# Counting matmuls that take four token tiles at once, and VectorE work moved into gaps, in an attention-plus-MoE kernel

## The chip, the cores and the metric

The kernel runs on one core of a Trainium2 chip. The metric is the device time of one execution in microseconds (us). Before the change it was run three times: 507.22, 510.45 and 506.15 us, median 507.22 us.

## The reference

The input is q, k and v for 4 batches, 8 heads, 768 positions and 64 dimensions. A token attends to a window of 31 positions around it and to the maxima and means of all 24 blocks of 32 keys and values. The result, 3072 tokens of 512 numbers, goes into a mixture of 8 experts in which every expert takes exactly 384 tokens:

```python
logits = x @ w_gate                        # 3072 x 8
for idx in np.argsort(-logits.flatten()):  # best pair first
    tok, e = idx // E, idx % E
    if assigned[tok] >= 0 or counts[e] >= cap:   # cap = 384
        continue
    assigned[tok] = e; counts[e] += 1
for e in range(E):
    out[assigned == e] = np.maximum(x[assigned == e] @ w1[e], 0.0) @ w2[e]
```

The greedy assignment is what makes the work sequential: which tokens an expert gets depends on which experts filled up before it.

## The kernel before, in words

**Stages.** Attention with its logits runs from the start to about 147 us. Then follow eight experts, one after another, each over the 384 tokens of the expert that fills up in that round. The order of the experts is thus found at run time: round r names the expert that is the next to fill up and the tokens it gets, and `widx` (where its weights lie) and `idx` (its token numbers) steer the loads of its weights and the gather of its tokens.

**A round** (`route`, L468). `aim` (L111) takes each token's best remaining logit (`best`), its expert (`oh`, one-hot) and a sortable integer `key`, all on VectorE, and `compare` (L103) makes the 0/1 table `g` of keys against 32 or 64 pivots. `search` (L444) then finds, digit by digit, the pivot at which the first expert reaches 384 tokens. For one digit it does: 24 counting matmuls on TensorE (L449; for each tile of 128 tokens, a 128-column slice of `g` is the stationary operand and the tile's 8 columns of `oh` move through, all added up in `pc`), a VectorE comparison with 384 (`full`, L451), one matmul with `steps` (L454), new pivots (L458) and the next `compare` (L460). A round has two searches of three digits, six digits in all, two of them of width 64 and four of width 32. Round 7, the last, needs no search. After the search come the running counts (`inc`, L508), a prefix matmul (`px`, L522), `place` (L529), the interval tables `span` (L546), 12 small matmuls (`at`, L554) and `idx` (L559). `spent` takes the tokens that are used up out of `WA`, and `close` (L510) takes the full expert out of the logits `L`.

**An expert** (`expert`, L738). Float32 products are made of three float32r products: each operand is split in a high part (ScalarE, `hi`, `xh`, `hh`) and a low part (VectorE, `lo`, `xl`, `hl`). 96 matmuls of 384 columns (L749) give `h`, 72 of 512 columns (L766) give `y`. The weights of the next expert are split in chunks of 128x1024 (`split_w`, L584; low part L594) and its gathered tokens are turned by TensorE in four `flip_x` (L614; the matmuls show as L135), each of which writes the one PSUM buffer `xt`, which is free again when ScalarE has read `xh` (L625) and VectorE `xl` (L628).

**What sets the order.** TensorE and VectorE each work through their instructions in the order in which the program issues them. That order is written by a small clock in the program: `spend` (L664) adds an estimate for each expert matmul to `now`; `service` issues the low parts that are due and then, if `ready` has come, lets `route` go on by one step (`advance`, L651). Each `yield` of `route` gives an estimate of the step's time on TensorE and of the VectorE work that must be over before the next step. So the matmuls of round r+1 are strewn among the matmuls of expert r and before. Rounds run ahead of the experts as far as these estimates let them. Low parts that are due go on the list `later` and are issued when their time has come, whatever VectorE is to do next. Round 0 (L705) runs by itself, before the first expert; three `advance` steps of round 1 stand between the turns of the first expert's tokens (L719).

```python
pc = R[:, :E]
for t in range(NT):                                       # L448
    nc.tensor.matmul(pc, g[t // HT][:, t % HT * n:t % HT * n + 128], oh[:, t], start=t == 0, stop=t == NT - 1)
full = rt.tile([128, E + 1], BF, name="full", bufs=2)
nc.vector.tensor_scalar(full[:, :E], pc, CAP - 0.5, 0.0, op0=OP.is_ge, op1=OP.max, accum_out=full[:, E:])
```

Of the 128 columns of the slice only the first n belong to tile t; the other rows of `pc` are not used.

Of the kernel before, what the change touches and what calls it, by code (L numbers as in the profile page):

```python
# [35 lines left out]
TUNE = dict(  # L36
    hop=0.22, dv=1.0, e5=2, e50=0, warm2=3.6192, adv=14, y0=2.6, y1=0.3, y2=0.45,
    y2m=0.021, y3=1.7, y4=1.5, y5=1.6, y7=1.1, lo=1.1, sp=1.6, qx=23.421, aw=9.0, as_=2.6,
# [18 lines left out]
def attention_moe(ctx, tc, qT, kT, v65, wg, w1r, w2r, cst, out, dbg=None, dbi=None):  # L57
# [14 lines left out]
    ids_b = cb[:, :2 * NT].rearrange("p (t k) -> p t k", k=2)  # L72
    steps = consts.tile([128, len(STEPS), 128], BF, name="steps")
    wgs = consts.tile([128, 4, E], F32, name="wgs")
    L = consts.tile([128, NT, E], F32, name="L")
# [34 lines left out]

    def aim(T, t0, t1, last=False):  # L111
        n = t1 - t0
        best, cand, tgt = T["best"][:, t0:t1], T["cand"][:, t0:t1], T["tgt"][:, t0:t1]
        nc.vector.tensor_reduce(best, L[:, t0:t1], axis=AX.X, op=OP.max)
        ranks, experts = [], [
            lambda: nc.vector.tensor_tensor(cand, L[:, t0:t1], best[:, :, None].to_broadcast([128, n, E]), op=OP.is_equal),
            lambda: nc.vector.tensor_tensor(cand, cand, WA[:, t0:t1], op=OP.mult),
            lambda: nc.vector.tensor_reduce(tgt, cand, axis=AX.X, op=OP.max),
            lambda: nc.vector.tensor_scalar(tgt, tgt, 0.5, None, op0=OP.max)]
        if not last:  # L120
            m, key = T["m"][:, t0:t1], T["key"][:, t0:t1]
            bits = T["best"].bitcast(I32)[:, t0:t1]
            ranks = [
                lambda: nc.vector.tensor_scalar(m, bits, 31, 0x7FFFFFFF, op0=OP.arith_shift_right, op1=OP.bitwise_and),
                lambda: nc.vector.scalar_tensor_tensor(key, bits, 0x8000, m, op0=OP.bitwise_xor, op1=OP.bitwise_xor),
                lambda: nc.vector.tensor_copy(T["dup"][:, t0:t1], T["halves"][:, t0:t1, 1:2].to_broadcast([128, n, 2])),
                lambda: compare(T["g"], T["dup"], T["piv"], T["digits"][0], t0, t1)]
            experts.append(lambda: nc.vector.tensor_tensor(T["oh"][:, t0:t1], cand, tgt[:, :, None].to_broadcast([128, n, E]), op=OP.is_equal))
        for pair in zip_longest(ranks, experts):
            for op in pair:  # L130
                if op:
                    op()

# [43 lines left out]
    with ExitStack() as att:  # L177
# [13 lines left out]

        nc.vector.memset(steps, 0.0)
        for i, (v, n) in enumerate(STEPS):
            nc.vector.memset(steps[:n, i], v)
# [22 lines left out]
        @task("tables", "pool", 3.5, ["constants2"], 1)  # L217
        def _():
            nc.gpsimd.tensor_copy(cb, XS[0][:, :TB])
            nc.gpsimd.tensor_copy(WA, w8f[:, None].to_broadcast([128, NT, E]))  # L220
            nc.gpsimd.tensor_copy(piv0, offs[:, :32])
            nc.gpsimd.tensor_copy(colsi, XS[0][:, TB:TW])
            nc.gpsimd.tensor_copy(pivw, offs[:, 128:192])

        def halves(t):
# [218 lines left out]
    def search(R, oh, dup, g, digits):  # L444
        below = -32768.0 - 65536.0 / digits[0]
        for i, n in enumerate(digits):
            pc = R[:, :E]
            for t in range(NT):  # L448
                nc.tensor.matmul(pc, g[t // HT][:, t % HT * n:t % HT * n + 128], oh[:, t], start=t == 0, stop=t == NT - 1)  # L449
            full = rt.tile([128, E + 1], BF, name="full", bufs=2)  # L450
            nc.vector.tensor_scalar(full[:, :E], pc, CAP - 0.5, 0.0, op0=OP.is_ge, op1=OP.max, accum_out=full[:, E:])  # L451
            yield 0.027 * NT, TUNE["y1"]
            ps = R[:, 16:17 + E]
            nc.tensor.matmul(ps, steps[:, STEP[digits][i]], full, start=True, stop=True)  # L454
            if i < 2:
                m = digits[i + 1]
                piv = rt.tile([128, 64], I16, name="piv", bufs=2)
                nc.vector.tensor_scalar(piv[:, :m], offs[:, FROM[digits][i]:FROM[digits][i] + m], ps[:, E:], below, op0=OP.add, op1=OP.add)  # L458
# [7 lines left out]
    ROUND = {}  # L466

    def route(r):  # L468
        T = first
        if r:  # L470
            T = targets(r)
            aim(T, 0, NT, r == E - 1)
            yield 0.0, TUNE["y0"]
        R = psum.tile([128, 512], F32, name="r")
# [40 lines left out]

        late = TUNE["e5"] if r else TUNE["e50"]
        if r < E - 1 and not late:
            close()
        ROUND[r] = [widx, None]
        yield 0.03, TUNE["y4"]  # L520
        px = R[:, 32:34]
# [9 lines left out]
        def spent():  # L531
            if r == E - 1:
                return
            if late == 1:
                close()
# [27 lines left out]
        if r < E - 1 and late == 2:  # L563
            close()
# [19 lines left out]
    def split_w(r, nm, j, n=1, wait=TUNE["wlo"]):  # L584
# [4 lines left out]
        for k in range(n):  # L589
            c = slice(k * 1024 // n, (k + 1) * 1024 // n)  # L590
            nc.scalar.activation(hi[:, c], raw[:, c], AF.Copy)  # L591

            def low(c=c):
                nc.vector.tensor_tensor(lo[:, c], raw[:, c], hi[:, c].bitcast(F32), op=OP.subtract)  # L594
# [18 lines left out]

    def flip_x(r, d):  # L614
        pt = psum.tile([128, 3, 128], F32, name="xt")
        for c in range(3):
            flip4(pt[:, c], XG[r, c][:, d * 128:(d + 1) * 128])
        split_x(r, d, pt)

    def split_x(r, d, pt):  # L620
# [6 lines left out]
        def low():  # L627
            nc.vector.tensor_tensor(xl[:, d], p, xh[:, d].bitcast(F32), op=OP.subtract)  # L628
            vector(0.55)
        later.append((state["now"] + TUNE["xlo"], low))  # L630

# [3 lines left out]

    def flush():
        for it in later[:]:
            later.remove(it)
            it[1]()

    def service():
        while True:
            for it in [x for x in later if x[0] <= state["now"]]:
                later.remove(it)
                it[1]()
# [92 lines left out]
    def expert(r):  # L738
# [3 lines left out]
        hl = ff.tile([128, 8, CAP], F32R, name="hl")  # L742
        for f in range(8):
            ph = psum.tile([128, CAP], F32, name="h", bufs=3)
            wh, wl = (w.rearrange("p (j d k) -> p j d k", j=2, d=4)[:, f % 2] for w in WT[r, "a", f // 2])
# [9 lines left out]
            def low(f=f, ph=ph):  # L755
                nc.vector.scalar_tensor_tensor(hl[:, f], ph, 0.0, hh[:, f].bitcast(F32), op0=OP.max, op1=OP.subtract)  # L756
                vector(0.55)
            later.append((state["now"] + TUNE["lo"], low))
            if f % 2 == 0:
                later.append((state["now"] + TUNE["sp"], lambda f=f: split_w(r, "b", f // 2)))  # L760
        py = [psum.tile([128, DM], F32, name="y", bufs=3) for c in range(3)]
# [84 lines left out]
```

## Time and profile before

| | us |
|---|---|
| device time of the profiled execution | 508.25 |
| its span, first to last instruction | 506.5 |
| so outside the span | 1.75 |
| median of the three runs | 507.22 |
| TensorE busy in the span | 463.3 |
| VectorE busy in the span | 330.1 |

The mean granted TensorE clock was 0.95 of full speed. In the views below a row of the timeline gives the start and the length in us, the engine, the line, the operation, what it writes and reads, how many instructions were merged, and in brackets how long the engine was idle before and what released it. A row of the chain gives start, length, engine, what is written, and line. Matmuls overlap: the time that one takes out of the stream is the difference of starts, not the length shown.

### The profile page before, as it was taken

What the parts mean: (1) busy time and instruction counts of PE and PEld (TensorE: products, weight loads), DVE (VectorE), ACT (ScalarE), POOL (GpSimd) and SP (SyncE); (2) the same over time, 40 slices, a digit from 0 to 9 for tenths busy, and PEclk for the clock granted to TensorE, in tenths of its full rate; (3) what the DMA queues carried; (4) which work ended last, traced back from release to release, by engine and by line L of the source; (5) the groups of instructions that cost most, each with busy time, mean ns of one, the idle gap of its engine ahead of it and who ended that gap; (6) DMA issues with size and microseconds to landing.
All of it is one profiled execution on the core that took longest, in us unless ns stands there. A gap on an engine that the chain in (4) does not pass through costs nothing.

```text
span 506.5 us, 13149 instructions
## 1 busy us (share of the span) xinstructions
PE 463.3 (91%) x5160; PEld 388.6 (77%) x5160; DVE 330.1 (65%) x1293; ACT 214.4 (42%) x450; POOL 131.7 (26%) x199
## 2 busy tenths in 40 slices
PE   3799999999973899989989999899999999999993
PEld 2568687877853798779768878877987998988982
DVE  3278789977866786757865966777778462362510
ACT  1277667876810441243323513342351453453410
POOL 9547743614220300220202302300400500402011
PEclk8799999999985699979998999999999999999997
DMA  8999969211110821920641733723535445531001
GB/s 264 315 303 297 320 221 312 91 51 44 65 65 6 295 96 38 323 98 1 231 167 63 249 146 104 272 84 154 180 109 184 127 162 169 180 111 42 22 21 41
DMA packets 24157, 76.28 MB, mean 151 GB/s; under 512 B 3488, under 2 KB 3744, under 8 KB 23712
## 3 DMA queue, kind: packets, MB, share of 16 engines
q1 hardware_dynamic: 18336, 56.58, 33.9%
q0 software_dynamic: 5760, 18.88, 10.7%
q8 instruction: 40, 0.66, 0.6%
q14 instruction: 21, 0.17, 0.1%
HBM read 62.86 MB, written 12.58 MB: 149 GB/s over the span
## 4 chain that ended last, share of the span: by engine, by line
PE 73%; DVE 13%; issue 7%; POOL 4%; DMA 1%; ACT 0%; POOLq 0%; SPq 0%; ACTq 0%; DVEq 0%
PE h L749 21%; PE y L766 19%; PE o L348 5%; PE t L135 5%; PE s L312 5%; PE r L449 5%; PE x L135 2%; PE x L269 2%; PE l L354 2%; PE xt L135 2%; POOL vw L204 2%; DVE al L594 2%; DVE g L107 2%; POOL out L732 1%; PE x L279 1%
## 5 line engine op out<-in xcount | busy, mean ns | idle before, releaser
L766 PE MATMUL y<-bl,hh 128*128 128x512 f32 x192 | 78.6, 409 | 0.0
L766 PE MATMUL y<-bh,hl 128*128 128x512 f32 x192 | 77.4, 403 | 0.0
L766 PE MATMUL y<-bh,hh 128*128 128x512 f32 x192 | 76.6, 399 | 0.0
L732 POOL DMA_INDIRECT out<-y,idx x24 | 23.9, 996 | 197.6 <-ACT y L730 193.4
L753 ACT ACTIVATE hh<-h 128x384 fp32r<-128x384 f32 x64 | 31.5, 492 | 89.7 <-PE h L749 88.9
L749 PE MATMUL h<-xh,ah 128*128 128x384 f32 x256 | 60.5, 352 | 1.3 <-DVE hl L756 1.3
L327 ACT ACTIVATE pe<-sm,mx 128x118 f32<-128x118 f32 x192 | 57.7, 384 | 8.3 <-DVE mx L320 8.1
L749 PE MATMUL h<-xh,al 128*128 128x384 f32 x256 | 58.1, 346 | 0.0
L749 PE MATMUL h<-xl,ah 128*128 128x384 f32 x256 | 56.8, 340 | 0.0
L756 DVE SCALAR_TENSOR_TENSOR hl<-h,hh 128x384 fp32r<-128x384 f32 x64 | 35.3, 552 | 30.9 <-ACT hh L753 30.9
L320 DVE CUSTOM_DVE_ANT_0 sm<-s,cs 128x118 f32<-128x118 f32 x192 | 41.6, 275 | 17.1 <-PE s L312 16.3
L605 POOL DMA_INDIRECT xg<-xd,idx x24 | 25.5, 1064 | 96.5 <-issue 67.5
L625 ACT ACTIVATE xh<-xt 128x384 fp32r<-128x384 f32 x28 | 13.8, 491 | 82.4 <-PE xt L135 82.4
L749 PEld LDWEIGHTS h<-xh,ah 128*128 128x128 f32 x256 | 46.2, 194 | 2.8 <-DVE hl L756 1.7
L591 ACT ACTIVATE ah<-raw 128x1024 fp32r<-128x1024 f32 (+1 forms) x36 | 32.7, 957 | 32.0 <-DMA raw<-w1r 29.4
L749 PEld LDWEIGHTS h<-xh,al 128*128 128x128 f32 x256 | 46.1, 193 | 0.0
L749 PEld LDWEIGHTS h<-xl,ah 128*128 128x128 f32 x256 | 45.3, 189 | 0.0
L449 PEld LDWEIGHTS <-g 128*128 128x128 bf16 x1008 | 28.8, 97 | 18.0 <-DVE g L107 7.6
L766 PEld LDWEIGHTS y<-bh,hh 128*128 128x128 f32 x192 | 36.4, 190 | 6.8
L766 PEld LDWEIGHTS y<-bh,hl 128*128 128x128 f32 x192 | 36.4, 190 | 5.7
L766 PEld LDWEIGHTS y<-bl,hh 128*128 128x128 f32 x192 | 36.2, 188 | 5.8
L594 DVE TENSOR_TENSOR al<-raw,ah 128x1024 fp32r<-128x1024 f32 (+1 forms) x36 | 38.7, 1099 | 2.5 <-ACT ah L591 2.5
(129 smaller groups left out, 789.5 us busy)
## 6 DMA issues: line engine op xcount, KB each, us to landing
raw<-w1r SPq DMA_DIRECT2D x32, 512.0 KB, 4.5
raw<-w2r SPq DMA_DIRECT2D x32, 512.0 KB, 4.3
vw<-v SPq DMA_DIRECT2D x48, 195.0 KB, 7.7
kd<-kT SPq DMA_DIRECT2D x16, 399.0 KB, 5.8
xd<-x POOLq DMA_DIRECT2D x24, 256.0 KB, 3.6
qt<-qT SPq DMA_DIRECT2D x3, 1536.0 KB, 9.8
qt<-qT SPq DMA_DIRECT2D x3, 512.0 KB, 5.5
xg<-xd,idx POOLq DMA_INDIRECT x24, 3.7
```

The costliest lines, as they stand in the source:

```text
L135: nc.tensor.transpose(o, i, idn)
L320: nc.vector.tensor_tensor_reduce(sm[:, p], PS[u][:, p], m, -0.125, 3e38, op0=OP.add, op1=OP.min, accum_out=mx[:, p:p + 1])
L327: nc.scalar.activation(PE_[u][:, p], SM[u][0][:, p], AF.Exp, bias=SM[u][1][:, p:p + 1], scale=-1.0)
L449: nc.tensor.matmul(pc, g[t // HT][:, t % HT * n:t % HT * n + 128], oh[:, t], start=t == 0, stop=t == NT - 1)
L591: nc.scalar.activation(hi[:, c], raw[:, c], AF.Copy)
L594: nc.vector.tensor_tensor(lo[:, c], raw[:, c], hi[:, c].bitcast(F32), op=OP.subtract)
L605: nc.gpsimd.indirect_dma_start(out=x, out_offset=None, in_=xd, in_offset=bass.IndirectOffsetOnAxis(ap=idx[:, c:c + 1], axis=0))
L732: st = nc.gpsimd.indirect_dma_start(out=out, out_offset=bass.IndirectOffsetOnAxis(ap=ROUND[r][1][:, c:c + 1], axis=0), in_=y, in_offset=None)
L749: nc.tensor.matmul(ph, a[:, d], b[:, d], start=n == 0, stop=n == 11)
L753: nc.scalar.activation(hh[:, f], ph, AF.Relu)
L756: nc.vector.scalar_tensor_tensor(hl[:, f], ph, 0.0, hh[:, f].bitcast(F32), op0=OP.max, op1=OP.subtract)
L766: nc.tensor.matmul(py[c], a[:, f, s], b, start=f == 0 and i == 0, stop=f == 7 and i == 2)
```

## The change

Four things are changed; arithmetic results stay the same.

- **Counting.** `many = 128 // n` tiles (four of width 32, two of width 64) share one counting matmul: the stationary slice holds their digit tables side by side and the 8 `many` columns of their `oh` move through. The sum `pb` has the wanted counts in its diagonal blocks. VectorE copies it to float16 (`part`), and `many` matmuls with a 0/1 table `same` pick the blocks and add them up in `pc`. Per digit there are 6 + 4 or 12 + 2 matmuls in place of 24, and one more VectorE step and one more `yield` between them.
- **The table `same`.** GpSimd clears it at the start, ahead of the two `VW` clears, and fills it with six copies in the task "tables".
- **Low parts.** An entry of `later` now has a cost, a slack and a tag. It is issued when it fits before `ready` plus 0.7 us, or when no round is under way, or when its slack is over (4.0 us for weights, 0.8 for tokens, 1.2 for `hl`). Low parts of weights are cut in halves of 512 columns. `flip_x` issues a waiting `xl` first, and expert step f a waiting `hl` of step f-3.
- **Next maxima in this tail.** `aim` is split in `aim_ranks` and `aim_experts`. Rounds 1 to 6 run `close` and `aim_ranks` of the next round right after `inc`, while the prefix matmul is due, and `spent` with `aim_experts` ahead of `span`; round 0 does all of it after its `idx`, where its `close` stood ahead of `place` before. A round then begins with its first count.

```diff
+    gap=0.7, ya=2.9, hop=0.22, dv=1.0, warm2=3.6192, ...
+    same = consts.tile([128, 6, 128], F16, name="same")
...
+        nc.gpsimd.memset(same, 0.0)
...
+            for k in range(2):
+                nc.gpsimd.tensor_copy(same[:, k, :64], idn[:, 64 * k:64 * k + 64])
+            for k in range(4):
+                nc.gpsimd.tensor_copy(same[:, 2 + k, :32], idn[:, 32 * k:32 * k + 32])
...
-            pc = R[:, :E]
-            for t in range(NT):
-                nc.tensor.matmul(pc, g[t // HT][:, t % HT * n:t % HT * n + 128], oh[:, t], start=t == 0, stop=t == NT - 1)
+            pc, many = R[:, :E], 128 // n
+            pb = R[:, 64:64 + many * E]
+            for t in range(0, NT, many):
+                nc.tensor.matmul(pb, g[t // HT][:, t % HT * n:t % HT * n + 128], oh[:, t:t + many].rearrange("p t e -> p (t e)"), start=t == 0, stop=t == NT - many)
+            part = rt.tile([128, 32], F16, name="part", bufs=2)
+            nc.vector.tensor_copy(part[:, :many * E], pb)
+            yield 0.03 * NT / many, TUNE["y1"]
+            for k in range(many):
+                nc.tensor.matmul(pc, same[:, many // 4 * 2 + k], part[:, k * E:(k + 1) * E], start=k == 0, stop=k == many - 1)
...
-            yield 0.027 * NT, TUNE["y1"]
+            yield 0.03 * many, TUNE["y1"]
...
-        T = first
-        if r:
-            T = targets(r)
-            aim(T, 0, NT, r == E - 1)
-            yield 0.0, TUNE["y0"]
+        T = AIMED.pop(r)
...
+        def turn():
             close()
+            AIMED[r + 1] = targets(r + 1)
+            aim_ranks(AIMED[r + 1], 0, NT, r + 1 == E - 1)
+        early = 0 < r < E - 1
+        if early:
+            turn()
...
-        yield 0.03, TUNE["y4"]
+        yield 0.03, TUNE["y4"], TUNE["ya"] if early else 0.0
...
             nc.vector.tensor_tensor(WA, WA, keep[:, :, None].to_broadcast([128, NT, E]), op=OP.mult)
+            aim_experts(AIMED[r + 1], 0, NT, r + 1 == E - 1)
+        if early:
+            spent()
...
-        if r:
-            spent()
-        yield 0.05, TUNE["y5"]
+        yield 0.05, TUNE["y5"] + (1.2 if early else 0.0)
...
         if r == 0:
+            turn()
             spent()
...
-        yield 0.45, TUNE["y7"]
+        yield 0.45, 0.0, TUNE["y7"]
...
-                later.append((state["now"] + wait, low))
+                for h in range(2):
+                    piece = slice(h * 512, h * 512 + 512)
+                    def half(piece=piece):
+                        nc.vector.tensor_tensor(lo[:, piece], raw[:, piece], hi[:, piece].bitcast(F32), op=OP.subtract)
+                        vector(0.61)
+                    later.append((state["now"] + wait, half, 0.61, 4.0, "w"))
...
     def flip_x(r, d):
+        flush("x")
...
+    def fits(it):
+        now, (due, _, cost, slack, _) = state["now"], it
+        idle = state["gen"] is None or not cost
+        return idle or now >= due + slack or max(state["dve"], now + TUNE["hop"]) + cost <= state["ready"] + TUNE["gap"]
```

More of the change, by code (lines that the diff above doesn't have):

```diff
@@ L36 @@
 TUNE = dict(
-    hop=0.22, dv=1.0, e5=2, e50=0, warm2=3.6192, adv=14, y0=2.6, y1=0.3, y2=0.45,
+    gap=0.7, ya=2.9, hop=0.22, dv=1.0, warm2=3.6192, adv=14, y0=2.6, y1=0.3, y2=0.45,
     y2m=0.021, y3=1.7, y4=1.5, y5=1.6, y7=1.1, lo=1.1, sp=1.6, qx=23.421, aw=9.0, as_=2.6,
@@ L109, in compare, with aim_ranks @@
                                         piv[:, None, :n].to_broadcast([128, b - a, n]).rearrange("p t (j k) -> p t j k", k=2), op=OP.is_ge)
-    def aim(T, t0, t1, last=False):
+    def aim_ranks(T, t0, t1, last=False):
         n = t1 - t0
-        best, cand, tgt = T["best"][:, t0:t1], T["cand"][:, t0:t1], T["tgt"][:, t0:t1]
+        best, cand = T["best"][:, t0:t1], T["cand"][:, t0:t1]
         nc.vector.tensor_reduce(best, L[:, t0:t1], axis=AX.X, op=OP.max)
[L115 to L119, printed above, removed]
         if not last:
@@ L122, in aim, with aim_experts @@
             bits = T["best"].bitcast(I32)[:, t0:t1]
[L123 to L132, printed above, removed]
+            nc.vector.tensor_scalar(m, bits, 31, 0x7FFFFFFF, op0=OP.arith_shift_right, op1=OP.bitwise_and)
+        nc.vector.tensor_tensor(cand, L[:, t0:t1], best[:, :, None].to_broadcast([128, n, E]), op=OP.is_equal)
+        if not last:
+            nc.vector.scalar_tensor_tensor(key, bits, 0x8000, m, op0=OP.bitwise_xor, op1=OP.bitwise_xor)
+            nc.vector.tensor_copy(T["dup"][:, t0:t1], T["halves"][:, t0:t1, 1:2].to_broadcast([128, n, 2]))
+            compare(T["g"], T["dup"], T["piv"], T["digits"][0], t0, t1)
+    def aim_experts(T, t0, t1, last=False):
+        n = t1 - t0
+        cand, tgt = T["cand"][:, t0:t1], T["tgt"][:, t0:t1]
+        nc.vector.tensor_tensor(cand, cand, WA[:, t0:t1], op=OP.mult)
+        nc.vector.tensor_reduce(tgt, cand, axis=AX.X, op=OP.max)
+        nc.vector.tensor_scalar(tgt, tgt, 0.5, None, op0=OP.max)
+        if not last:
+            nc.vector.tensor_tensor(T["oh"][:, t0:t1], cand, tgt[:, :, None].to_broadcast([128, n, E]), op=OP.is_equal)
+    def aim(T, t0, t1):
+        aim_ranks(T, t0, t1)
+        aim_experts(T, t0, t1)
     def flip4(o, i):
@@ L466, in attention_moe @@
     ROUND = {}
+    AIMED = {0: first}
     def route(r):
-        T = first
-        if r:
-            T = targets(r)
-            aim(T, 0, NT, r == E - 1)
-            yield 0.0, TUNE["y0"]
+        T = AIMED.pop(r)
         R = psum.tile([128, 512], F32, name="r")
@@ L514, in close @@
             nc.vector.tensor_tensor(L, L, pen[:, None].to_broadcast([128, NT, E]), op=OP.add)
-        late = TUNE["e5"] if r else TUNE["e50"]
-        if r < E - 1 and not late:
+        def turn():
             close()
+            AIMED[r + 1] = targets(r + 1)
[3 more added lines that the diff above has]
+            turn()
         ROUND[r] = [widx, None]
-        yield 0.03, TUNE["y4"]
+        yield 0.03, TUNE["y4"], TUNE["ya"] if early else 0.0
         px = R[:, 32:34]
@@ L533, in spent @@
                 return
-            if late == 1:
-                close()
             keep = rt.tile([128, NT], F32, name="keep", bufs=2)
@@ L560, in route @@
         if r == 0:
+            turn()
             spent()
         ROUND[r][1] = idx
-        if r < E - 1 and late == 2:
-            close()
         if dbi is not None:
@@ L629, in low @@
             vector(0.55)
-        later.append((state["now"] + TUNE["xlo"], low))
+        later.append((state["now"] + TUNE["xlo"], low, 0.55, 0.8, "x"))
     scat = []
@@ L634, in attention_moe, with flush @@
     later = []
-    def flush():
+    def flush(tag=None):
         for it in later[:]:
-            later.remove(it)
-            it[1]()
+            if tag is None or it[4] == tag:
+                later.remove(it)
+                it[1]()
+    def fits(it):
+        now, (due, _, cost, slack, _) = state["now"], it
+        idle = state["gen"] is None or not cost
+        return idle or now >= due + slack or max(state["dve"], now + TUNE["hop"]) + cost <= state["ready"] + TUNE["gap"]
     def service():
         while True:
-            for it in [x for x in later if x[0] <= state["now"]]:
-                later.remove(it)
-                it[1]()
+            for it in [x for x in later if x[0] <= state["now"] and fits(x)]:
+                if fits(it):
+                    later.remove(it)
+                    it[1]()
             if state["done"] < E - 1 and state["ready"] <= state["now"]:
@@ L743, in expert @@
         for f in range(8):
+            flush(("h", f - 3))
             ph = psum.tile([128, CAP], F32, name="h", bufs=3)
@@ L757, in low @@
                 vector(0.55)
-            later.append((state["now"] + TUNE["lo"], low))
+            later.append((state["now"] + TUNE["lo"], low, 0.55, 1.2, ("h", f)))
             if f % 2 == 0:
-                later.append((state["now"] + TUNE["sp"], lambda f=f: split_w(r, "b", f // 2)))
+                later.append((state["now"] + TUNE["sp"], lambda f=f: split_w(r, "b", f // 2), 0.0, 0.0, "b"))
         py = [psum.tile([128, DM], F32, name="y", bufs=3) for c in range(3)]
```

## The prediction

> **What bounds the kernel now.** I read the page's busy shares first, then the experts in a table of windows, then what TensorE waited for in them, then TensorE's timeline around one count.
>
> ```profile
> PE 463.3 (91%) x5160; PEld 388.6 (77%) x5160; DVE 330.1 (65%) x1293; ACT 214.4 (42%) x450; POOL 131.7 (26%) x199
> ...
> 174.00:221.00 47.00, 44.54 (x396) 37.39 (x394) 35.46 (x111) 17.65 (x29) 5.60 (x9) 0.94 0.46 170
> 221.00:266.00 45.00, 42.41 (x347) 36.01 (x346) 31.28 (x99) 15.69 (x24) 4.33 (x7) 0.96 0.35 121
> 266.00:310.00 44.00, 43.78 (x419) 36.81 (x418) 31.37 (x105) 15.38 (x24) 7.44 (x11) 0.97 0.38 132
> 310.00:353.50 43.50, 41.91 (x362) 35.03 (x362) 33.83 (x122) 15.13 (x23) 6.74 (x11) 1.00 0.48 168
> 353.50:395.40 41.90, 40.79 (x348) 34.52 (x347) 31.68 (x107) 15.41 (x24) 6.83 (x11) 1.00 0.47 153
> 430.30:463.50 33.20, 33.20 (x176) 30.25 (x176) 15.53 (x20) 14.10 (x22) 6.11 (x10) 1.00 0.36 111
> ```
>
> The windows' columns are: stretch, length, busy time of TensorE, its weight load, VectorE, ScalarE, GpSimd, granted clock, DMA share, GB/s. Each window is one expert. The one at 430 us has no routing beside it and takes 33.2 us. The first five, with rounds 1 to 7 strewn in, take 42 to 47 us, and TensorE is busy in all but 0.2 to 2.6 us of each. So TensorE's stream is the bound here, and what leaves the stream leaves the time. The idle times add up to 8.0 us; the waits name most of them:
>
> ```profile
> PE xt L135 <- DVE xl L628: 6.2, 6, 2.2
> PE h L749 <- DVE hl L756: 1.3, 1, 1.3
> ```
>
> Seven waits, 7.5 us, and in all of them TensorE stands before a PSUM buffer whose low part VectorE has not yet read. The price of a count is in the stream:
>
> ```profile
> 186.12 0.51 PE L749 MATMUL h<-xh,al 128*128 128x384 f32 x2
> 186.48 0.76 PE L449 MATMUL r<-oh,g 128*128 128x8 bf16 x24
> 187.10 0.60 PE L749 MATMUL h<-xh,al 128*128 128x384 f32 x2
> 187.54 0.34 PE L749 MATMUL h<-xl,ah 128*128 128x384 f32 x1
> 187.72 0.18 PE L454 MATMUL r<-full,steps 128*128 128x9 bf16 x1
> 187.75 0.78 PE L749 MATMUL h<-xl,ah 128*128 128x384 f32 x3
> ...
> 202.46 0.46 PE L554 MATMUL r<-place,span 128*128 128x25 f16 x12
> 202.77 0.48 PE L766 MATMUL y<-bh,hh 128*128 128x512 f32 x1
> ```
>
> From start to start, 24 counting matmuls take 0.62 us, 25.8 ns each. Two `h` matmuls before them take 0.36 us, the two behind 0.44: going back to float32r costs some 0.09 us. Twelve matmuls with 25 moving columns take 0.31 us, again 25.8 ns, so columns are free from 8 to 25.
>
> **The count, in the experts: -8.2 us.** For 32 moving columns I take 25.8 ns too; by the `h` rows a column costs 0.17 us / 384 = 0.45 ns, so 32 of them (14 ns) lie below that step. A digit of width 32 goes from 24 matmuls to 6 + 4: 14 x 0.0258 = 0.36 us less, and a second block in the stream adds a switch of 0.09: -0.27. One of width 64 goes to 12 + 2: -0.26 + 0.09 = -0.17. A round: 4 x 0.27 + 2 x 0.17 = 1.42. Rounds 1 to 6: 8.5; round 1's first digit is counted before expert 0: 8.2 us. If the second switch costs 0.2 it is 4.2, if nothing 11.4.
>
> **The new step on VectorE: 0 on the path.** TensorE does other expert matmuls while `part` is copied, if the copy comes within the 0.22 + 0.30 us that the program's clock leaves.
>
> ```profile
> L451 DVE TENSOR_SCALAR_CACHE_REDUCE full<-r 128x8 bf16<-128x8 f32 x42 | 6.9, 165 | 32.7 <-PE r L449 32.5
> L458 DVE TENSOR_SCALAR piv<-cs,r 128x32 int16<-128x32 f32 x14 | 3.4, 246 | 5.4 <-PE r L454 5.4
> L594 DVE TENSOR_TENSOR bl<-raw,bh 128x1024 fp32r<-128x1024 f32 x32 | 38.9, 1216 | 0.0
> L594 DVE TENSOR_TENSOR al<-raw,ah 128x512 fp32r<-128x512 f32 x8 | 5.0, 682 | 1.3 <-ACT ah L591 1.3
> ```
>
> The copy lies between 0.16 and 0.25 us by the first two rows. Behind it stand the comparison, then the pivots; in front of it a half of a low part can stand, 0.68 us. If that cover is gone, TensorE waits up to 0.68 us at each of 36 hops (a rival). Cutting the weights in halves costs 2 x 0.682 - 1.216 = 0.15 us a chunk. VectorE in the five windows was busy 163.6 of 221.4 us, 74%; with 36 copies (6) and some 40 cut chunks (6) it is about 176 of 210, 83%: hidden, with less room.
>
> **Round 0, alone on the path: +1.5 us, of which about 0 arrives.**
>
> The rows are of the chain, the last one of VectorE's timeline:
>
> ```profile
> 151.37 0.37 DVE g L107
> 151.74 0.05 issue
> 151.78 0.82 PE r L449 x24
> 152.62 0.19 DVE full L451 x2
> ...
> 158.25 1.03 DVE g L107 x2
> 159.35 0.48 PE r L449 x12
> ...
> 151.37 0.63 DVE L107 TENSOR_TENSOR g<-dup,piv 128x384 bf16<-128x384 int16 x2
> ```
>
> Here the count starts after the first half of `g`; from the start of `g` to its end is 1.24 us. Six matmuls must still wait for the second half of `g` (0.63), then three of them (some 0.25 with latencies), a hop and copy (0.03 + 0.17 + 0.04) and four more matmuls (0.26): 1.4 us, +0.2 a digit. The last, of width 64: 0.31 + 0.45 against 0.48, +0.27; the first, whose counts mostly ran ahead, +0.43. Together +1.5 us (0.9 to 1.9). What follows takes it back (rows of the timeline, and at the end the gathers of this stretch among the DMA issues, with the us to landing):
>
> ```profile
> 161.84 0.36 DVE L514 TENSOR_TENSOR L<-L,pen 128x192 f32<-128x192 f32 x1
> 162.52 0.41 DVE L529 SCALAR_TENSOR_TENSOR place<-inc,r,ge 128x24 f16<-128x24 bf16 x2 [0.32 <-issue]
> 168.19 1.37 POOL L605 DMA_INDIRECT xg<-xd,idx  x1 [0.30 <-issue]
> 169.86 0.34 DVE L114 TENSOR_REDUCE best<-L 128x24 f32<-128x192 f32 x1
> 172.42 0.76 PE L449 MATMUL r<-oh,g 128*128 128x8 bf16 x24 [1.25 <-DVE oh L128]
> 173.03 0.88 PE L135 MATMUL y<-cs,xg 128*128 128x128 f32 x3
> ...
> xg<-xd,idx POOLq DMA_INDIRECT x3, 3.5
> ```
>
> `close` leaves the way to `place` (-0.5), so the gathers come 1.0 us later. But the third turn of the first tokens stood at 173.03 behind a count that waited for `aim` (169.86 to 172.37), behind the weights' low parts. Now `aim` runs while the first weights travel, and the third gather (168.2 + 1.0 + 3.5 to landing, about 172.7) releases the turn. I take 0, between -0.5 and +1.5.
>
> **GpSimd at the start: +0.7 us.** Three rows of the chain, three of GpSimd's timeline:
>
> ```profile
> 0.74 2.97 POOL g L97 x4
> 3.72 10.46 POOL vw L204 x2
> 14.18 1.45 POOL kw L173 x2
> ...
> 23.80 0.29 POOL L222 CAST colsi<-x 128x128 int16<-128x128 f32 x1
> 24.04 0.24 POOL L223 CAST pivw<-cs 128x64 int16<-128x64 f32 x1
> 25.74 1.13 POOL L173 COPY kw<-kd 128x1128 f32<-128x1128 f32 x1 [1.47 <-DMA kd<-kT]
> ```
>
> The chain starts on GpSimd: clears back to back, then the first window copies, for which TensorE waits. Clearing `same` (768 columns) costs 768/832 of 0.74: +0.7 us, at most that, at least 0. The six small copies (about 0.2 us each, 1.3 in all) fall into the 1.47 us in which GpSimd waits for a load: 0.
>
> **The stalls: -4.1 us.** What is late is a token low part behind a whole weight part or behind a search step that itself waits for TensorE:
>
> ```profile
> 213.66 1.22 DVE L594 TENSOR_TENSOR al<-raw,ah 128x1024 fp32r<-128x1024 f32 x1
> 215.49 0.52 PE L135 MATMUL xt<-cs,xg 128*128 128x128 f32 x3 [1.29 <-DVE xl L628]
> 264.08 0.52 PE L135 MATMUL xt<-cs,xg 128*128 128x128 f32 x3 [2.21 <-DVE xl L628]
> ...
> 211.00:223.00 12.00, 9.54 (x62) 7.19 (x62) 7.52 (x16) 5.32 (x9) 2.91 (x5) 0.77 0.55 208
> 262.00:270.00 8.00, 5.92 (x46) 5.05 (x47) 3.39 (x13) 2.06 (x4) 3.12 (x5) 0.79 0.18 68
> ```
>
> At the ends of experts 0 and 1 the turns are crowded, because `idx` came late in the expert. The granted clock falls there too (0.77 and 0.79): at half clock for 0.42 of 8 us, 3.4 us, the same work loses about 1.7 us; the window at 211 by the same count 2.8, part of it while idle: I take 2.3. In the changed kernel a round starts at once with its count (`aim` was 2.6 us of planned VectorE time) and a low part no longer delays a search step by 1.2 us; against this stand one more hop a digit and some 3 us more of VectorE ahead of `idx` (`close`, and `aim` in its two parts). I get `idx` of round 1 about 1 us earlier and that of round 2 about 5 us earlier. So expert 0 keeps its crowd; expert 1 loses its waits (2.21 + 0.23) and its 1.7 us of clock: 4.1. The bounds are 0 and all of it, 7.5 + 4.0 = 11.5. The Trainium skill ("TensorE: Matmul & The Clock Gate", section "HAM oscillation — how this bites in real kernels") says that the clock falls after gaps of more than about 3.4 us; the trace shows it falling behind waits of at most 2.21 us. By the page nothing but the waits could be won back, 7.5 us in place of 11.5, and 2.4 in place of my 4.1.
>
> **Sum.** 506.5 + 0.7 + 0 - 8.2 - 4.1 = 494.9 us of span; with the 1.75 us outside it 496.65, against 508.25 for the same execution, 11.6 us less. That execution lay 1.0 above the median of 507.22. Against the median: **495.6 us**. A measurement of this kernel can tell about 1%, 5 us, from no change.
>
> **Rivals.**
> 1. *The count is saved, the stalls are not* (0.12). The slack limits issue most low parts where they stood. 507.2 - 8.2 + 0.7 = 499.7. For it: VectorE is at 83%, gaps are few. Against: a half fits behind nearly every step by the 0.7 us.
> 2. *Experts 0 and 1 stay tied to the routing* (0.14). If the added hops and the longer way to `idx` keep `idx` where it was, gather and turns end these two experts, and only rounds beside the other experts pay: 8.2 x 4/6 = 5.5; with +0.7 and half of the bound of +1.5 on the first turns, 507.2 - 4.0 = 503.2. For it: turns at the very end in both. Against: round 2 starts 3 us earlier.
> 3. *All waits and clock slips go* (0.14). 507.2 - 8.2 - 11.5 + 0.7 = 488.2. For it: every wait is for a low part, and these are now cut, tagged and placed. Against: in expert 0 the cause is the gather's time.
> 4. *The new hop becomes the wait* (0.08), on the other side. TensorE takes its instructions in order, so a copy of `part` that finds a half of a weight part (0.68 us) before it holds the whole stream at the `same` matmuls. At one of two hops that is 18 x 0.68 = 12.2 us: 507.2 + 0.7 - 8.2 + 12.2 and +1.0 of clock = 512.9. It turns the sign once a hop waits more than (8.2 - 0.7) / 36 = 0.2 us. For it: the 0.7 us by which a half may pass `ready`. Against: TensorE never waited in the experts for `full` (L451), which has the same cover now.
>
> **How the numbers follow.** My forecast has 0.52, with a range of its own of 492 to 501; the others as above. Faster by over 1% (below 502.1): 0.52 + 0.12 + 0.14 = 0.78; within 1%: 0.14; slower: 0.08. The range of 488 to 504 holds the forecast and rivals 1 to 3 and leaves out rival 4.
>
> **What would show it.** The counting line has 336 matmuls and the selecting line 140, where 1008 stood; a count of width 32 moves the stream by 0.16 us and its selection by 0.10. Experts 2 to 4 shrink by about 1.4 us each, expert 1 by 5. The first window copy on GpSimd starts at 14.9. The waits for `xl` are 3 to 4 us. The forecast is wrong if TensorE waits for `part`, if 32 columns cost more than 26 ns, or if expert 1 still ends in crowded turns.

## The result and the profile after

| | before | after |
|---|---|---|
| median, us | 507.81 (4 runs, 506.15 to 510.45) | 605.43 (4 runs, 604.94 to 605.63) |
| profiled execution, us | 508.25 | 604.94 |
| span, us | 506.5 | 602.9 |

The ratio is 1.1915, 95% interval 1.1862 to 1.1969: the kernel is 98 us slower. One run further down (552.97 us at a clock of 0.81, where the seven others of its kernel took 521 to 526 us) is left out of its kernel's time. The first part of the page after, with the lines of TensorE's busy tenths and granted clock:

```profile
span 602.9 us, 12161 instructions
PE 482.0 (80%) x4628; PEld 388.7 (64%) x4628; DVE 345.6 (57%) x1395; ACT 212.7 (35%) x450; POOL 130.8 (22%) x206
PE   2899999998379969976994599359935993599994
PEclk9999999999579977995997599769975997599998
```

TensorE has 532 instructions fewer and 19 us more of busy time, and it is idle for 121 us where it was idle for 43. The two rows of tenths show a pattern with a period of four slices (60 us) from the middle on: two slices at 9, then a 3 or 4 and a 5, with the clock down in the same slices. That is once per expert. The experts, in a table of windows with the columns of the prediction's (the edges are rough: experts 1 to 5 really start at 228.8, 282.1, 340.2, 400.8 and 461.1 us):

```profile
176.00:229.00 53.00, 46.42 (x288) 36.10 (x287) 33.71 (x120) 17.90 (x29) 5.41 (x9) 0.87 0.45 161
229.00:283.00 54.00, 44.32 (x262) 35.55 (x261) 29.96 (x100) 15.58 (x25) 6.62 (x10) 0.85 0.31 108
283.00:344.00 61.00, 46.90 (x274) 38.15 (x273) 33.37 (x108) 15.39 (x24) 7.34 (x12) 0.81 0.28 99
344.00:405.00 61.00, 43.95 (x270) 34.68 (x268) 31.75 (x108) 14.94 (x23) 6.37 (x10) 0.82 0.28 96
405.00:466.00 61.00, 43.92 (x269) 35.05 (x270) 31.93 (x109) 14.94 (x23) 6.38 (x10) 0.83 0.28 96
```

From start to start, experts of 42 to 47 us have become experts of 52 to 61, although each window has some 80 to 145 matmuls fewer. What TensorE waited for from 170 to 600 us (total, times, longest):

```profile
PE xt L140 <- DMA xg<-xd,idx: 39.9, 18, 7.0
PE xt L140 <- DVE xl L651: 25.1, 18, 2.3
PE r L571 <- DVE span L565: 12.6, 4, 4.0
PE r L465 <- DVE part L462: 1.2, 1, 1.2
```

The added step `part`, which I had feared as a wait on the chip, holds TensorE once, for 1.2 us. The big waits are those for the gather of the next expert's tokens (`xg`), for the low parts between the turns (`xl`), and for `span`, the last step before the gather: for everything that lies between the end of a round and the start of the expert that it names. TensorE's timeline over one such stretch, from the last matmul of expert 2 to the first ones of expert 3 (in brackets how long TensorE had been idle, and what ended it):

```profile
321.34 0.39 PE L797 MATMUL y<-bh,hh 128*128 128x512 f32 x1
323.89 0.62 PE L571 MATMUL r<-place,span 128*128 128x25 f16 x12 [2.16 <-DVE span L565]
329.94 0.45 PE L140 MATMUL xt<-cs,xg 128*128 128x128 f32 x1 [5.44 <-DMA xg<-xd,idx]
331.26 0.48 PE L140 MATMUL xt<-cs,xg 128*128 128x128 f32 x1 [0.87 <-DMA xg<-xd,idx]
332.69 0.48 PE L140 MATMUL xt<-cs,xg 128*128 128x128 f32 x1 [0.95 <-DMA xg<-xd,idx]
334.34 0.90 PE L140 MATMUL xt<-cs,xg 128*128 128x128 f32 x3 [1.17 <-DVE xl L651]
337.55 0.90 PE L140 MATMUL xt<-cs,xg 128*128 128x128 f32 x3 [2.31 <-DVE xl L651]
339.63 0.90 PE L140 MATMUL xt<-cs,xg 128*128 128x128 f32 x3 [1.17 <-DVE xl L651]
340.18 0.67 PE L780 MATMUL h<-xh,ah 128*128 128x384 f32 x1
```

Expert 2 has ended at 321.7, and 18.5 us pass until expert 3 begins. In them TensorE is idle for 14.1 us (the brackets added up) and does the twelve `at` matmuls of round 3 and the twelve turns, nothing of an expert. Such a stretch is called a hand-over below. What sets the pace is in the chain of work that ended last (start, length, what):

```profile
318.68 0.36 DVE best L115
...
323.13 0.24 DVE span L565
...
329.02 3.62 DMA xg<-xd,idx
...
333.69 2.83 ACT ah L607 x3
...
339.57 4.81 DVE al L617 x8
```

Tail of the round on VectorE (with the next round's maxima in it), gather, turns among ScalarE's weight splits, and eight halves of the weights' low parts at the new expert's start: each waits for the one ahead. The prediction's windows of before have TensorE busy in all but 0.2 to 2.6 us of an expert.

So the experts have caught up with the routing. `prepare` says what happens then: once `q`, which counts the 24 groups of three `y` matmuls, is above `qx` = 23.42, that is behind the last matmul of expert r, and round r+1 has no `idx` yet, it calls `advance` until the round is over, and fetches, turns and splits behind it. The eight `idx` of each kernel, first and last:

```profile
L559 DVE TENSOR_REDUCE idx<-hit x8: 230/231/232, 165.0 to 397.8; 128x3 int32<-128x75 f32 x8
```

```profile
L576 DVE TENSOR_REDUCE idx<-hit x8: 230/231/231, 168.7 to 539.7; 128x3 int32<-128x75 f32 x8
```

The seven rounds behind round 0 took 232.8 us before and 371.0 after. The lead of a round is how far its end lies ahead of the start of the expert that it names. To see it apart from the stalls, I counted in TensorE's timeline how many of the 168 matmuls of each expert were issued ahead of the twelve `at` matmuls of a round. In experts (0.73: in expert 0, behind 73% of its matmuls; a whole number: behind the end of an expert, by force):

| round | 1 | 2 | 3 | 4 | 5 | 6 |
|---|---|---|---|---|---|---|
| before | 0.73 | 1.62 | 2.36 | 3.13 | 3.95 | 4.78 |
| after | 0.88 | 1.96 | 3.00 | 4.00 | 5.00 | 6.00 |

Before, a round used up 0.74 to 0.89 of an expert's matmuls, so the lead grew from 0.27 to 1.2 experts. After, round 2 uses 1.08; from round 3 on every round is finished by force at the end of an expert, and the lead stays at nothing.

### The profile page after: what moved, and what is told of

Its sections match the earlier page's. It is cut to its first block, busy times and chain, and to the rows that moved or that the text cites. A ratio compares the mean times of both kernels' runs of the same rounds, so it can differ in the third digit from the quotient of the medians.

```text
span 602.9 us, 12161 instructions
## 1 busy us (share of the span) xinstructions
PE 482.0 (80%) x4628; PEld 388.7 (64%) x4628; DVE 345.6 (57%) x1395; ACT 212.7 (35%) x450; POOL 130.8 (22%) x206
## 4 chain that ended last, share of the span: by engine, by line
PE 57%; issue 15%; DVE 13%; POOL 5%; ACT 4%; DMA 4%; POOLq 0%; DVEq 0%; ACTq 0%
PE h L780 18%; PE y L797 15%; PE t L140 4%; PE o L358 4%; PE s L322 4%; DMA xg<-xd,idx 4%; ACT ah L607 3%; DVE al L617 2%; PE xt L140 2%; PE x L140 2%; PE l L364 2%; PE x L279 2%; POOL vw L210 2%; POOL out L762 1%; DVE xl L651 1%
## 5 line engine op out<-in xcount | busy, mean ns | idle before, releaser
L140 PE MATMUL xt<-cs,xg 128*128 128x128 f32 x87 | 27.1, 412 | 65.0 <-DMA xg<-xd,idx 39.9
L780 PE MATMUL h<-xl,ah 128*128 128x384 f32 x256 | 62.7, 359 | 3.1 <-DVE xl L651 2.2
L780 PE MATMUL h<-xh,ah 128*128 128x384 f32 x256 | 64.9, 371 | 0.2 <-ACT xh L176 0.2
L140 PEld LDWEIGHTS xt<-cs,xg 128*128 128x128 f32 x87 | 14.2, 193 | 77.1 <-DVE xl L651 29.9
L780 PE MATMUL h<-xh,al 128*128 128x384 f32 x256 | 61.7, 362 | 0.0
L651 DVE TENSOR_TENSOR xl<-xt,xh 128x384 fp32r<-128x384 f32 x28 | 15.6, 556 | 65.6 <-ACT xh L648 65.6
L330 DVE CUSTOM_DVE_ANT_0 sm<-s,cs 128x118 f32<-128x118 f32 x192 | 41.5, 275 | 19.6 <-PE s L322 18.7
L780 PEld LDWEIGHTS h<-xl,ah 128*128 128x128 f32 x256 | 48.5, 201 | 5.3 <-DVE xl L651 4.0
L780 PEld LDWEIGHTS h<-xh,ah 128*128 128x128 f32 x256 | 49.5, 207 | 1.2 <-ACT xh L176 1.0
L780 PEld LDWEIGHTS h<-xh,al 128*128 128x128 f32 x256 | 49.6, 206 | 0.0
L617 DVE TENSOR_TENSOR bl<-raw,bh 128x512 fp32r<-128x512 f32 x64 | 43.0, 683 | 0.0
```

What stands on the lines that cost most here:

```text
L140: nc.tensor.transpose(o, i, idn)
L330: nc.vector.tensor_tensor_reduce(sm[:, p], PS[u][:, p], m, -0.125, 3e38, op0=OP.add, op1=OP.min, accum_out=mx[:, p:p + 1])
L617: nc.vector.tensor_tensor(lo[:, piece], raw[:, piece], hi[:, piece].bitcast(F32), op=OP.subtract)
L780: nc.tensor.matmul(ph, a[:, d], b[:, d], start=n == 0, stop=n == 11)
```

## The experiments

**The theories.** The one that I held (A in the expectations) is that the added step costs nothing on the chip but much in the program's own clock. `advance` plans each step of VectorE with 0.22 us of hop and 0.30 us (`y1`), behind whatever low parts are planned already, and only then lets the round go on, so a third step per digit lets more expert matmuls pass; a round gets longer than an expert, and the lead is gone. Its first rivals laid the loss on one of the other parts: B on the low parts, which now wait for gaps and come late, C on the tail, which now carries `close` and the next maxima ahead of `idx`. The first four runs take one or two of the three parts out; the kernel before ran on the same chip in 506.97 us (7 runs). The positions in the expectations follow from the order in which the program issues its instructions, so it proves nothing that the timelines agree with them; what a run tests is the time.

All these kernels are the changed program with parts switched off by three flags (`COUNT`, `GAPS`, `TAIL`), and the diffs are cut and against the changed kernel. Even with every flag at 0 a waiting `xl` is issued ahead of a turn and a waiting `hl` of step f-3 ahead of step f; no run has that alone.

**Count alone.** Undone are the gaps (low parts issued when due, whole) and the tail (`aim` at the head of a round):

```diff
+COUNT, GAPS, TAIL = 1, 0, 0
...
-        T = AIMED.pop(r)
+        if TAIL or not r:
+            T = AIMED.pop(r)
+        else:
+            T = targets(r)
+            aim_old(T, 0, NT, r == E - 1)
+            yield 0.0, TUNE["y0"]
...
-        idle = state["gen"] is None or not cost
+        idle = state["gen"] is None or not cost or not GAPS
```

> Only the new counting with its extra step; low parts and the maxima of the next round as before the change. Theory A (the rounds lose their lead: with the extra step a round takes longer than an expert in the program's own clock, so every expert ends in turns and gathers that wait for its successor's idx): in the order in which the instructions are issued, idx of rounds 1 to 6 stands 0.86, 1.97, 3.00, 4.00, 5.00 and 6.00 experts after the start of expert 0, so it should be as slow as the changed kernel, 590 to 610 us. Rival B (low parts held back for gaps starve the experts): without them the counting should show its gain, 497 to 502 us. Rival C (the longer way to idx by maxima and spent ahead of span): likewise 497 to 502 us.

Measured: 603.99 us (one run), the whole loss. Its waits look like those of after:

```profile
PE xt L164 <- DMA xg<-xd,idx: 45.2, 14, 8.6
PE xt L164 <- DVE xl L697: 22.1, 20, 1.5
```

Rounds 1 to 6 end at 0.86, 1.97, 3, 4, 5 and 6 experts. The counting part by itself is enough for the loss; rivals B and C, which lay it on the gaps or the tail, fall.

**Without the count.** The old 24 matmuls and two steps per digit, with gaps and tail:

```diff
+COUNT, GAPS, TAIL = 0, 1, 1
...
-            for t in range(0, NT, many):
+            if not COUNT:
+                for t in range(NT):
+                    nc.tensor.matmul(pc, g[t // HT][:, t % HT * n:t % HT * n + 128], oh[:, t], start=t == 0, stop=t == NT - 1)
+            for t in range(0, NT, many) if COUNT else ():
```

> The other two parts without the new counting: 24 matmuls for each digit, low parts in gaps, next maxima in the tail. Theory A: idx of rounds 1 to 6 at 0.74, 1.54, 2.39, 3.27, 4.07 and 4.80 experts, so the lead grows as before the change: 498 to 506 us. Rival B and rival C: still slow, 560 to 605 us.

Measured: 525.0 us, ratio 1.0337 (1.0266 to 1.0409). The collapse is gone (rounds end at 0.74, 1.54, 2.39, 3.27 experts), but this missed my expectation by some 20 us: gaps and tail, which I had as a gain, are a loss of their own. Its waits:

```profile
PE xt L164 <- DVE xl L697: 9.9, 9, 2.5
PE h L826 <- DVE hl L833: 8.7, 4, 3.3
```

They are for low parts that come late: the tokens', as before but more of them, and `hl`, for which TensorE waited once and 1.3 us before.

**Count and tail; count and gaps.** The other two pairs, by the same flags.

> New counting and next maxima in the tail, low parts issued whole and when due, as before the change. Theory A: idx at 0.93, 2.00, 3.00, 4.00, 5.00 and 6.00 experts: 595 to 612 us. Rival B: 497 to 502 us. Rival C: about 605 us.

> New counting and low parts in gaps, the maxima of a round at its own start as before the change. Theory A: idx at 0.80, 1.88, 2.98, 4.00, 5.00 and 6.00 experts, slow but a little later to fall into step: 585 to 605 us. Rival B: about 605 us. Rival C: 497 to 502 us.

Measured: 607.97 and 591.59 us (one run each). With the count in, the other two parts move the time by a few per cent. The second, without the long tail, is 14 us faster than the full change. Some 5 us of that are hand-overs: those behind experts 2 to 5 take 18.3 to 18.7 us in it and 18.5 to 20.4 in the full change. Another 6 us are in experts 0 and 1, and open.

The next four runs shared another chip, on which the kernel before took 519.2 us (17 runs); their ratios are to that. Their expectations in us were written for the first chip, so the ratio times 507 is what to hold against them.

**A head start.** The full change, with nine more steps of round 1 issued before expert 0. It asks whether the loss is a lead that ran out:

```diff
+LEAD = 9
...
+    for _ in range(LEAD):
+        advance()
```

> The changed kernel with nine more steps of round 1 taken before expert 0; every later instruction of a round is the same. In the order of issue idx of rounds 1 to 6 then stands at 0.58, 1.61, 2.61, 3.61, 4.65 and 5.66 experts, in place of 0.88, 1.96, 3.00, 4.00, 5.00 and 6.00. Theory A (lost lead): the waits for the gather vanish, 510 to 535 us, some 9 us of it for the steps that nothing hides. Rival D (the added steps cost TensorE their time in the experts, whatever the lead): 585 to 610 us.

Measured: 529.35 us (one run), against 519.2 for before, a ratio of 1.02 (517 us on the first chip's scale). Expert 0 starts at 185.3 in place of 177.2 us, which is paid once; then no round is forced. Rounds end at 0.58, 1.61, 2.61, 3.61, 4.65 and 5.66 experts: each uses 1.00 to 1.04 of an expert, and the lead is nearly the same at the end as after round 2. With the same instructions and 8 us spent up front the loss is 10 us where it was 98. What is left is waiting for late low parts in the stream (total, times, longest):

```profile
PE h L829 <- DVE hl L836: 14.1, 9, 2.3
PE xt L165 <- DVE xl L698: 8.1, 13, 1.7
```

**Gaps alone, tail alone.** To split what the run without the count had lost.

> Only the low parts in VectorE's gaps, in halves; 24 counting matmuls, maxima at the start of a round. idx at 0.67, 1.40, 2.18, 2.97, 3.75 and 4.56 experts. If the 18 us of the run without the counting come from the tail (theory E: the block of maxima and spent ahead of span holds up the hl and xl behind it): 499 to 507 us. If they come from held-back low parts (rival F): 515 to 527 us.

> Only the next maxima in the tail. idx at 0.80, 1.61, 2.46, 3.33, 4.21 and 5.02 experts. Theory E: 515 to 527 us, with waits for hl and xl of 15 us or more. Rival F: 503 to 510 us.

Measured: gaps 522.71 us (7 runs), ratio 1.008 (1.0041 to 1.0119); tail 530.06 us, ratio 1.0248 (1.0201 to 1.0295). On the first chip's scale that is 511 and 519.5 us: the tail is the bigger part, as in theory E, but the gaps cost more than E had for them. Their waits, gaps first:

```profile
PE xt L164 <- DVE xl L697: 9.1, 7, 2.2
PE r L499 <- DVE full L496: 7.7, 4, 3.6
```

```profile
PE h L826 <- DVE hl L833: 8.7, 5, 2.7
PE xt L164 <- DVE xl L697: 8.2, 7, 2.0
```

With the gaps, a count's comparison comes up to 3.6 us late; with the tail, `hl` comes late (5 waits, 8.7 us), and `hl` and `xl` together make the 15 us or more that E asked for. That it is the block of maxima in the tail (planned with 2.9 us at once) that keeps `hl` waiting is argued from the order of issue, not shown by a run of its own.

**Count and gaps, with a shorter planned wait.** If the loss is the planned time and not the chip's, planning less should win it back with the same instructions:

```diff
+COUNT, GAPS, TAIL = 1, 1, 0
+TUNE['y1'] = 0.0
```

> New counting and gaps, maxima at the start of a round, and the program's wait for the two short VectorE steps of a digit (part, full) set from 0.3 to 0 us, so that only its 0.22 us for the hop is left. Theory A: idx at 0.72, 1.52, 2.26, 3.04, 3.82 and 4.62 experts, about as before the change, so the counting can show its gain less some waits of TensorE for part and full (at most 0.15 us at each of 72): 495 to 506 us. Rival D: 585 us or more.

Measured: 515.57 us, ratio 0.995 (0.991 to 0.9989; 504.5 us on the first chip's scale), where the same kernel with `y1` at 0.3 had taken 591.59 on the other chip. Rounds end at 0.72, 1.52, 2.26, 3.04 experts. TensorE's waits for the copy come to 2.1 us and for the comparison to nothing that shows, so little of the 0.30 us was needed here:

```profile
PE xt L165 <- DVE xl L698: 10.3, 8, 2.8
PE r L495 <- DVE part L492: 2.1, 1, 2.1
```

The last four shared the same chip again (before 518.95 us, 12 runs).

**The step without the gain.** The kernel before with its 24 matmuls, and only a third VectorE step and its `yield` added in each digit. It tells the wait from the counting matmuls:

```diff
+            if not COUNT:
+                part = rt.tile([128, 32], F16, name="part", bufs=2)
+                nc.vector.tensor_copy(part[:, :E], pc)
+                yield 0.027 * NT, TUNE["y1"]
...
-            yield 0.03 * many, TUNE["y1"]
+            yield (0.03 * many if COUNT else 0.12), TUNE["y1"]
```

> The kernel before with one thing added: a digit keeps its 24 counting matmuls, but VectorE copies the count and the program waits a third time before it goes on, as the new counting does; TensorE gains nothing and the experts don't get shorter. idx of rounds 1 to 6 at 0.83, 1.90, 2.96, 4.00, 5.00 and 6.00 experts. Theory A in its narrow form (the third wait of a digit alone loses the lead): 90 to 115 us more than before on the same chip. Rival G (the lead is lost because the experts became shorter by the matmuls saved): at most 15 us more.

Measured: 601.07 us (one run), 82 us more than before: a little under what I expected of theory A, and far from rival G, by which the saved matmuls lose the lead and the wait by itself costs 15 us at most. Nothing reads the copy's result. Rounds end at 0.83, 1.90, 2.96, 4, 5 and 6 experts, and the waits are after's:

```profile
PE xt L164 <- DMA xg<-xd,idx: 42.1, 15, 9.2
PE xt L164 <- DVE xl L701: 26.0, 20, 3.2
```

**Count alone with the short wait, its control, and a later flush.** The first is the count part with `y1` at 0, the second the same without the count (a control: the kernel before with `y1` at 0, but for the two low parts named above), the third count and gaps with `y1` at 0, in which the waiting halves are flushed one by one ahead of the expert step that reads them and not all at an expert's start (the cut lines do the same for the second weights and for `hl`):

```diff
-                later.append((state["now"] + wait, half, 0.61, 4.0, "w"))
+                later.append((state["now"] + wait, half, 0.61, 4.0, ("w", r, nm, j)))
...
+            flush(("w", r, "a", f // 2))
```

> Only the new counting, with the wait for part and full at 0 instead of 0.3 us. idx at 0.75, 1.70, 2.59, 3.36, 4.17 and 5.06 experts. Theory A: out of lockstep, 0 to 2% below before on the same chip (8 us of matmuls saved, a few us of waits for the crowded turns of experts 1 and 2). Rival D: 15% or more above.

> The kernel before with the wait for full at 0 instead of 0.3 us and nothing else; idx at 0.64, 1.33, 2.01, 2.79, 3.48 and 4.14 experts. It says how much of the two short-wait kernels comes from the wait itself: if the gain is the counting's, this one lies within 0.5% of before or above it; if the wait is what helps, 1% or more below.

> New counting, gaps, short wait, and at the start of an expert only the low parts of its first weight chunk are forced out, the others just before their use (before: all of them, up to eight halves, 4.9 us of VectorE ahead of the next search step). idx at 0.72, 1.49, 2.23, 3.03, 3.77 and 4.62 experts. If the backlog at the expert's start is what still costs: 1 to 2.5% below before on the same chip; if not, as the kernel without it, 0 to 1% below.

Measured: 504.98 us, ratio 0.9712 (0.9659 to 0.9764); 512.94 us, ratio 0.9868 (0.9813 to 0.9924); 519.18 us, ratio 1.0001 (0.997 to 1.0032). The first beats both kernels, by more than I expected. Of its 14.0 us the shorter planned wait is worth 6.0 (the two forced low parts named above are in it too) and the count another 8.0. The control's 1.3% says by its own expectation that the wait helps. Windows of the first for experts 1 to 3, its waits, and a wait of the control:

```profile
222.00:265.20 43.20, 40.32 (x274) 32.60 (x272) 31.98 (x103) 15.38 (x24) 5.88 (x9) 1.00 0.38 133
265.20:305.80 40.60, 39.99 (x281) 32.62 (x279) 31.57 (x106) 15.60 (x24) 5.90 (x9) 1.00 0.40 139
305.80:347.70 41.90, 40.66 (x284) 32.79 (x281) 32.19 (x110) 15.12 (x23) 6.59 (x11) 1.00 0.39 139
```

```profile
PE xt L165 <- DVE xl L698: 6.5, 7, 1.4
PE r L495 <- DVE part L492: 0.4, 1, 0.4
```

```profile
PE r L500 <- DVE full L497: 7.0, 7, 1.6
```

With the counting matmuls of the changed kernel these experts take 41 to 43 us in place of 53 to 61, at the full clock. The control waits for `full` instead (7.0 us in all, 7 times): with two steps per digit and no time planned for them, TensorE sometimes gets to the result of the comparison too early.

The third was a miss: I had held the eight halves at an expert's start for what the gaps still cost, and spreading them won nothing (1.0001, against 0.995 with the halves at the start). That the gaps cost something beside the count is measured (0.995 against 0.971, in two groups on one chip); by what, is in part open. More than half lies in one place: of the 13.0 us between the spans of the two profiled executions (514.8 and 501.8), 7.6 are in expert 3, which takes 49.5 us at a clock of 0.90 with the halves at the start and 41.9 at 1.00 in the last window above. With the later flush it takes 50.8 at 0.93.

```profile
311.20:360.70 49.50, 44.62 (x293) 35.74 (x291) 36.37 (x135) 15.17 (x24) 7.00 (x11) 0.90 0.46 160
```

TensorE is idle there for 4.9 us, 2.8 of them in one wait for `xl`. That this wait brings the lower clock is argued, not shown; why the low part is late just there is open.

## Why the prediction was wrong

I said 495.6 us with a range of 488 to 504, and 0.08 for slower; it is 605.4.

**The step that failed is "The stalls: -4.1 us"**, in its reckoning of when `idx` comes: "I get `idx` of round 1 about 1 us earlier and that of round 2 about 5 us earlier", against which I had put "one more hop a digit" as a small debit. In VectorE's timeline of before and of after the `idx` of rounds 1 and 2 stand at:

```profile
203.56 0.23 DVE L559 TENSOR_REDUCE idx<-hit 128x3 int32<-128x75 f32 x1
246.37 0.23 DVE L559 TENSOR_REDUCE idx<-hit 128x3 int32<-128x75 f32 x1
```

```profile
212.51 0.23 DVE L576 TENSOR_REDUCE idx<-hit 128x3 int32<-128x75 f32 x1
266.49 0.23 DVE L576 TENSOR_REDUCE idx<-hit 128x3 int32<-128x75 f32 x1
```

Round 1's came 9.0 us later, round 2's 20.1. I had priced the hop in time on TensorE, where it is nearly free, and not in the lead of the rounds. From the table of positions: a round used 0.81 of an expert on average before (rounds 2 to 5) and uses 1.02 with the head start, where nothing is forced. That is 0.21 x 168, some 35 expert matmuls more per round, 6 for each hop; at the program's estimates (0.174 and 0.228 us) 1.2 us a hop. Of these 0.52 are the hop and `y1`; that the rest is low parts planned ahead of the step is argued. The head start has gaps and tail too. The control and the count with the short wait differ in the count alone: a round uses 0.71 and 0.86 of an expert there, 4 matmuls or 0.8 us more for each hop, with nothing planned for `y1`. With `y1` at 0.3 a round of six digits then lasts longer than an expert. The count alone and the step without the gain show that this suffices; the head start and the two kernels with the count and a short wait show that it is lead and planned time, not anything the chip is slow at.

**The forced end was not worked out.** Rival 2, "Experts 0 and 1 stay tied to the routing", named the place and had 503.2. It took the crowded turns of before for the worst that can happen, and only for two experts. The code that I had read has a cliff: past `qx` the rest of a round, the gather, the turns and the splits are issued in series, 18.5 us in the timeline above. And the state keeps itself up: a round that ends by force leaves the next one to begin with the next expert, and it is again a little longer than that. Experts 0 to 6 grew by 4.6, 7.9, 14.1, 17.5, 18.4, 25.6 and 5.0 us.

**The count, -8.2 us: right, where the lead is kept.** 8.0 us between the control and the count with the short wait, on one chip. That it agrees so closely is in part luck: this difference also holds 1.7 us by which the count starts expert 0 later, and the two kernels' different waits (7.0 us for `full` in one, 6.5 for `xl` in the other). The price itself is in TensorE's timeline of after:

```profile
293.49 0.32 PE L460 MATMUL r<-oh,g 128*128 128x32 bf16 x6
293.65 0.78 PE L780 MATMUL h<-xh,ah 128*128 128x384 f32 x3
294.98 0.26 PE L465 MATMUL r<-part,same 128*128 128x8 f16 x4
295.10 0.94 PE L780 MATMUL h<-xl,ah 128*128 128x384 f32 x4
```

Six matmuls of 32 columns move the stream by 0.16 us, the four selections by 0.12 (I had 0.16 and 0.10). With the two switches of 0.09 a digit of width 32 saves 0.25 us (I had 0.27), one of width 64, by the same timeline at 300.2 and 301.7 us (0.31 and 0.07), some 0.15 (I had 0.17). Over the 35 digits that makes 7.6 us.

**VectorE's new step, 0 on the path: nearly right on the chip.** There is one wait of 1.2 us for `part` in after; the two kernels with gaps and a short wait have 2.1 and 4.5 us of them. Rival 4 was the only one that forecast a loss, and its sign was right by luck: in its mechanism the copy holds TensorE, whereas the loss came by the program's clock, which is there to prevent just that.

**Round 0, +1.5 of which about 0 arrives, and GpSimd, +0.7: too low.** The first window copy on GpSimd starts at 14.86 (I said 14.9). But the last group of logits matmuls, which starts at 146.03 before, starts at 146.89 with count or count and gaps, 147.07 with the tail alone, 148.98 with gaps and tail and 148.12 with everything: the tail's part of this was not in the sum, and why it comes is open. In the run of count and gaps `idx` of round 0 is 1.7 us further from that group than before (20.7 against 19.0), near my +1.5. Most of it arrived: expert 0 starts at 174.07 before, at 176.20 with count and gaps and at 177.24 with everything, 3.2 us later, against 0.7 in my sum.

**The rest of the stalls: wrong in sign.** Gaps and tail, to which I gave 4.1 us of gain, lose 0.8% and 2.5% by themselves. Rivals 1 and 3, which asked only how much of that gain comes, lie on the wrong side. Of the signs of being wrong that I had named, two came: TensorE waited for `part`, if only once, and expert 1 ended in crowded turns.

**One length.** The 33.2 us of the expert without routing are the length of the window that I had set; from start to start it takes 34.5. No term hangs on it.

## What to carry to other kernels

When the order of two streams is written by a clock in the program, each added step must be priced twice: in the engine's time, and in how far the stream that it belongs to falls behind; compare the length of a round with the length of what it must stay ahead of, before and after. Read out of the code what happens when the lead reaches zero, since past that point the loss isn't a few stalls but a serial hand-over each time. When such a step is added, set its planned wait anew: here the count alone took 1.19 times the kernel before with 0.3 us in one estimate, and 0.97 times with 0.

## What the runs showed of the hardware that I had not expected

- The kernel before took 506.97 us on one chip and 518.95 to 519.2 on another (7, 12 and 17 runs), 2.4% apart. So each kernel is held against the runs of before on its own chip.
- The granted clock is low in every hand-over of the changed kernel, 0.50 to 0.62 over the six. The window of the one shown:

```profile
321.70:340.20 18.50, 4.42 (x26) 2.63 (x25) 5.29 (x18) 6.23 (x9) 5.12 (x8) 0.59 0.72 256
```

  It is 0.59 there and 0.81 to 0.87 over whole experts, so that 92 matmuls fewer in the window of expert 3 show as more busy time: 43.95 us (x270) after, 41.91 (x362) before at 1.00.
- Going from 8 to 32 moving columns changes nothing that the trace can show: six such matmuls move the stream by 0.16 us, 27 ns each with the rounding of the rows, beside 25.8 ns at 8 columns.
